# Fourth quarter of Q by seven-product runs, reciprocals of the attention denominator spread earlier, six output stores issued by ScalarE

## The chip, the cores and the metric

The kernel runs on one core of one Trainium2 chip. A core has five engines that run their own instruction streams in order: TensorE (PE; its weight loads are shown as PEld), VectorE (DVE), ScalarE (ACT), GpSimd (POOL) and SyncE (SP). They share an on-chip memory (SBUF), a set of accumulation banks that PE writes (PSUM) and 16 DMA engines. The metric is the device time of one execution in microseconds, the median of several executions; lower is better.

## The reference, cut to what matters

The input x has 2048 tokens of 1024 features, in bfloat16. The first block is linear attention with 32 heads of 32 features after a layer norm; the second is a token mixer, a two-layer MLP over the token axis with 3584 hidden units.

```python
def _A_ref(x, wqkv, wo):                       # x is layer-normed
    qkv = ((x @ wqkv).reshape(B, S, 3, H, Dh)).transpose(2, 0, 3, 1, 4)
    q, k, v = qkv[0], qkv[1], qkv[2]
    phi = lambda t: jnp.where(t > 0, t + 1, jnp.exp(t)) + 1e-6
    pq, pk = phi(q), phi(k)
    kv = jnp.einsum("bhsd,bhse->bhde", pk, v)
    z = jnp.einsum("bhsd->bhd", pk)
    num = jnp.einsum("bhqd,bhde->bhqe", pq, kv)
    den = jnp.einsum("bhqd,bhd->bhq", pq, z)[..., None] + 1e-6
    return (num / den).transpose(0, 2, 1, 3).reshape(B, S, D) @ wo
...
h = x + _A_ref(_layernorm(x), A_wqkv, A_wo)
h2 = h + _B_ref(_layernorm(h), B_w1, B_b1, B_w2, B_b2)   # norm, w1 over tokens, gelu, w2, transpose
```

So each token's phi(q) is needed, and a reciprocal of one denominator per token and head.

## The kernel before, in words

All large products use a seven-product scheme for two-by-two blocks (in the manner of Strassen and Winograd): four products' worth of sums of blocks are made on DVE, and PE does seven block products in place of eight. Where it isn't used, a plain product is done.

**Keys, values, queries.** The tokens are taken in eight pairs of 128 (`q` from 0 to 7). For each pair there is a key run and a value run (`KRun`, `VRun`): seven products of four matmuls of 512 columns each. `run_step` interleaves a run with the end of the previous one. The queries are kept transposed, 1024 features by tokens, in `pqT`; the tokens are cut in four quarters `u` of 512, and the features in eight groups `j` of 128. One *unit* (u, j) is a plain product: eight matmuls of 512 columns, then phi, which is an exponential and a relu on ACT and two instructions on DVE (`phi_evac`). Quarter 2 alone is done by two seven-product runs (`QRun`, halves 0 and 1), set between the key and value runs of pair 5; each of their seven products is eight matmuls of 256 columns. The other 24 units are plain: eight of them are placed among the key and value runs and right after them (`q_fill`), the other 16 in the loop over `q_units[8:]`.

**The loop over the left units.** With index n it does one unit a pass (`q_held`), and beside it: `kv_transpose` and `fold(j)`, which multiply the key-value matrix of each head into the output weights `wo_sb` (two matmuls a pass, evacuated by ACT and DVE); `den(u)`, eight small matmuls whose result is the denominators of a quarter, then a logarithm and an exponential on ACT, which write the reciprocals into the one buffer `rd_sb`, and a store of it to DRAM (`rd_dram`); `den_spread(u)`, eight DMAs that read it back, each to 32 partitions, four for the half h=0 of the features and four for h=1, into one of three buffers (`thirds`); `scale_q(u, h)`, one DVE instruction that multiplies phi(q) of half a quarter by the reciprocals; and the first sums of the mixer (`first_sums`), which need the mixer's first weights (`load_w1(0, ...)`, two loads of 1 MB). The dictionaries `den_at`, `spread_at`, `scale_at` and `sums_at` say at which n each stands.

**The output blocks.** For each of the 16 blocks of 128 tokens, `seed(i+1)` copies x into two PSUM banks, `out_mm(i)` adds sixteen matmuls of 512 columns (its weights are the scaled `pqT`), and `out_evac(i)` copies the sum to SBUF, takes the statistics of the next layer norm on DVE and stores the block. `h_scale`, `normalize_h` and `combine_h` prepare the mixer's operands. A block's eight weight loads for j = 0 to 7 come in order, j = 0 to 3 from the half h=0 of a quarter, j = 4 to 7 from h=1.

**What sets the order.** Most of this stretch is written out by hand (`pin`, and the wrappers `hv`, `ht`, `hs`, `hd`, which hold an instruction of DVE, PE, ACT or SP in program order). The rest is placed by a scheduler at build time. In the compiled order every DMA that SP or ACT issues gets one of eight completion counters (DMAHW0 to DMAHW7), given out in turn over both queues in the scheduler's order; a DMA isn't issued before the previous DMA on its counter has landed, and until then all that follows on its queue waits too.

Of the kernel before, what the change touches and what calls it, by code (L numbers as in the profile page):

```python
# [10 lines left out]
P = 128  # L11
# [19 lines left out]
def kernel(  # L31
# [751 lines left out]
    with ExitStack() as actx:  # L783
# [26 lines left out]
        with ExitStack() as a1:  # L810
# [11 lines left out]
            later = [pqT[:, j:j + 4, u * SW:(u + 1) * SW].bitcast(FP16) for u, j in ((1, 0), (NSC - 1, 0), (NSC - 1, 4))]  # L822
# [485 lines left out]
            q_units = [(u, j) for u in (0, 1, NSC - 1) for j in range(ND)]  # L1308
# [28 lines left out]
            for q in range(2, NVP):  # L1337
                runs = [KRun(q), VRun(q)]
                if q == 5:
                    runs = [runs[0], QRun(q // 2, 0), runs[1], QRun(q // 2, 1)]  # L1340
                for n in runs:
# [11 lines left out]
                    def after5():  # L1353
                        if kind == "V":
                            kv_accum(2 * q - 2)
                            kv_accum(2 * q - 1)
                        if i < NS:
                            ln_finish(i)
                            load_next(i + 2)

                    def after7():
                        if kind == "V" and q != 5 and q + 1 < NVP:
                            x_sums(q + 1)
                        if kind == "Q" and n.half == 1:
                            x_sums(q + 1, slice(0, 3))
# [10 lines left out]
            q_fill()  # L1376
            kv_accum(NS - 2)
            kv_accum(NS - 1)
            for n in range(3):
                q_fill()  # L1380
# [29 lines left out]
        ndp = a3p.enter_context(tc.tile_pool(name="ndp", bufs=3, space=PSUM))  # L1410
        rd_dram = [dram.tile([P, SW], FP16, name=f"rd_dram{u}") for u in range(NSC)]

        with ExitStack() as a3:
# [17 lines left out]
            SPREAD = (0, 2, 1, 3)  # L1431
            NH = ND // 2

            def den_mm(u):
                ps = ndp.tile([P, SW], F32, tag="den", name="den_ps")
                for o in range(2):
                    for g in range(4):
# [5 lines left out]
                            start=(o == 0),  # L1443
                            stop=(o == 1),
# [5 lines left out]
            def den_inv(u, ps):  # L1450
                hs.activation(ps[:], ps[:], ACT.Ln, bias=eps_den[:], scale=1.0 / S)
                hs.activation(rd_sb, ps[:], ACT.Exp, scale=-1.0)
                hd.dma_start(rd_dram[u][:], rd_sb)

            def den_spread(u):
                rows = rd_dram[u].rearrange("(g o h) n -> o h g n", g=4, h=HB)
                for h in range(2):
# [8 lines left out]
            def den(u):  # L1466
                den_inv(u, den_mm(u))
# [37 lines left out]
            def place(i):  # L1505
                u, r = divmod(i, NSC)
                return i if u != 2 else NSC * u + r % 2 * 2 + r // 2

            def out_mm(i):
                at = place(i) * P  # L1510
                for dc in range(NDC):
# [10 lines left out]
            def out_evac(i):  # L1522
# [8 lines left out]
                hd.dma_start(o_dram[i * P:(i + 1) * P, :], h_bf[:])  # L1531
# [17 lines left out]
            for half in range(2):  # L1549
                load_w1(0, half, pin)  # L1550
            for i in range(XRL + 1):
                load_xr(i)

            def first_sums():
                cur = Quad([Mixer1(0), Mixer1(1)])
                for m in (5, 6, 7, 3):
# [4 lines left out]
                Held.on = False  # L1561
                yield cur
# [3 lines left out]
            sums_at, ahead = (4, 8, 9, 11, 13), first_sums()  # L1566
            scale_at = {5: (0, 0), 6: (0, 1), 10: (2, 0), 12: (2, 1), 15: (1, 0)}
            den_at = {0: 0, 2: 2, 9: 1}
            spread_at = {0: 0, 6: 2, 12: 1}
            kv_transpose()  # L1570
            for n, (u, j) in enumerate(q_units[8:]):
                if n == len(q_units) - 8 - 1:
                    seed(0)
                q_held(u, j)
                if 1 <= n < 1 + ND:
                    fold(n - 1)
                if n in den_at:
                    den(den_at[n])
                if n in spread_at:
                    den_spread(spread_at[n])  # L1580
                if n in (12, 13):
                    load_w1(1, n % 2, pin)
                if n in scale_at:
                    scale_q(*scale_at[n])
                if n in sums_at:
                    cur = next(ahead)
# [10 lines left out]
            scale_at = {0: (1, 1), 6: (3, 0), 8: (3, 1)}  # L1597
# [243 lines left out]
```

## Time and profile before

| | |
|---|---|
| median of 3 runs | 558.95 us (558.83 to 558.98) |
| profiled execution | 559.43 us, of which the instructions span 557.7 us |
| busy share of the span | PE 99%, DVE 80%, PEld 57%, ACT 52%, POOL 5% |
| chain that ended last | PE 91%, DMA 4%, DVE 2%, ACT 1% |
| loop over the 16 left units | 143.3 to 177.2 us |
| output blocks | 177.2 to 233.1 us |
| granted clock | 1.0 of full speed throughout |

The span is cut at times counted from its first instruction. A busy share is an average over stages; a stage is read from its own windows. The start of a matmul group, less the start of the group before it, is the time that the earlier one held PE (the durations printed overlap, since matmuls are pipelined).

### The profile page before, as it was taken

How to read it: one execution, taken by the hardware profiler on the slowest of the kernel's cores; microseconds unless marked ns; L12 is line 12 of the kernel's file. 1: busy time of each engine (PE TensorE's matmuls, PEld its weight loads, DVE VectorE, ACT ScalarE, POOL GpSimd, SP SyncE). 2: the span in 40 equal slices, each digit the busy share in tenths (PEclk: the TensorE clock that was granted, in tenths of full speed). 3: DMA queues.
4: the chain of work that ended last, by engine and by line, in shares of the span. 5: the costliest groups of instructions: out<-in, count | busy, mean ns of one | idle time of the engine just before them, and what ended most of it. 6: DMA issues, size and time to landing. Idle time of an engine off the chain costs nothing.

```text
span 557.7 us, 8915 instructions
## 1 busy us (share of the span) xinstructions
PE 550.7 (99%) x3370; PEld 320.4 (57%) x3387; DVE 443.8 (80%) x858; ACT 288.8 (52%) x614; POOL 26.2 (5%) x36
## 2 busy tenths in 40 slices
PE   8999999999999999999999999999999999999997
PEld 3444446645444444456766767666444667667665
DVE  6898888754488688889989789887996879749747
ACT  5747678665776877646556465464210412413311
POOL 1000000000000000000000000000003103103111
PEclk9999999999999999999999999999999999999999
DMA  8933341202966961102250440413769659849434
GB/s 297 308 76 76 80 89 22 39 0 72 317 155 192 316 196 75 76 0 90 64 152 4 148 133 21 150 43 91 202 204 237 190 137 242 209 126 240 94 106 75
DMA packets 83931, 74.51 MB, mean 134 GB/s; under 512 B 15650, under 2 KB 76336, under 8 KB 83888
## 3 DMA queue, kind: packets, MB, share of 16 engines
q1 hardware_dynamic: 79504, 69.87, 42.0%
q0 software_dynamic: 4096, 3.68, 5.0%
q8 instruction: 26, 0.43, 0.3%
q10 hardware_dynamic: 288, 0.39, 0.2%
q14 instruction: 17, 0.14, 0.1%
HBM read 59.12 MB, written 11.67 MB: 127 GB/s over the span
## 4 chain that ended last, share of the span: by engine, by line
PE 91%; DMA 4%; DVE 2%; ACT 1%; SPq 1%; issue 0%; DVEq 0%; ACTq 0%
PE psI L234 23%; PE psC L234 14%; PE acc_t L234 14%; PE psB L234 8%; PE psC L966 4%; PE psB L966 4%; PE psA L966 4%; PE acc_t L888 3%; PE acc_t L1298 2%; PE psB L346 2%; PE psA L346 2%; PE psE L966 2%; PE psC L346 2%; DMA wq<-in_B_w_dram 2%; DMA wkv<-in_A_wqkv_dram 1%; PE kvps L917 1%
## 5 line engine op out<-in xcount | busy, mean ns | idle before, releaser
L234 PEld LDWEIGHTS <-is 128*128 128x128 f16 x736 | 71.8, 98 | 31.3 <-DVE is L234 0.4
L234 PEld LDWEIGHTS <-sa 128*128 128x128 f16 x606 | 59.2, 98 | 27.5 <-issue 0.3
L234 PEld LDWEIGHTS <-wq 128*128 128x128 bf16 (+1 forms) x496 | 48.5, 98 | 28.1 <-issue 1.2
L234 PE MATMUL acc_t<-wo_sb,pqT 128*128 128x512 f16 x256 | 55.6, 379 | 0.0
L491 POOL DMA_DIRECT2D out_dram<-wq x28 | 24.3, 927 | 519.6 <-ACT wq L494 487.7
L234 PEld LDWEIGHTS <-pqT 128*128 128x128 bf16 x256 | 25.0, 98 | 30.5 <-issue 0.6
L234 DVE TENSOR_TENSOR t<-psI,t 128x256 f32<-128x256 f32 (+1 forms) x45 | 20.8, 475 | 22.2 <-PE psI L234 21.0
L194 DVE TENSOR_SCALAR e_sb<-e_sb 128x512 bf16<-128x512 bf16 x64 | 18.4, 287 | 21.8 <-ACT e_sb L189 21.6
L234 PE MATMUL psC<-gs,wq 128*128 128x512 f16 x140 | 34.1, 379 | 0.0
L966 PEld LDWEIGHTS <-xs 128*128 128x128 f16 x208 | 20.1, 98 | 22.1 <-DVE xs L955 0.6
L234 PE MATMUL psC<-hT,sa 128*128 128x512 f16 x112 | 31.2, 379 | 0.0
L234 PE MATMUL psI<-hi,is 128*128 128x256 f16 x200 | 30.0, 273 | 0.0
L234 PE MATMUL psB<-hT,sa 128*128 128x512 f16 x112 | 29.7, 379 | 0.0
L234 PE MATMUL acc_t<-xnT,wq_sb 128*128 128x512 bf16 x125 | 29.3, 379 | 0.3
L189 ACT ACTIVATE e_sb<-acc_t 128x512 bf16<-128x512 f32 x32 | 19.1, 598 | 18.6 <-PE acc_t L1298 10.0
L234 DVE BATCH_NORM_STATS2 hst<-acc_t 128x6 f32<-128x512 f32 x32 | 21.4, 691 | 9.1 <-ACT h_bf L234 8.9
L966 PE MATMUL psA<-wkv,xnT 128*128 128x512 bf16 x98 | 26.2, 379 | 0.3
L966 PEld LDWEIGHTS <-xnT 128*128 128x128 bf16 x156 | 15.2, 98 | 18.1 <-issue 0.2
L234 PE MATMUL psC<-hT,wq 128*128 128x512 f16 x96 | 24.6, 379 | 0.0
L234 ACT CAST h_bf<-acc_t 128x512 bf16<-128x512 f32 x32 | 18.4, 582 | 12.0 <-PE acc_t L234 12.0
L234 DVE TENSOR_TENSOR e<-psI,es 128x256 f32<-128x256 f32 x20 | 8.5, 424 | 19.9 <-PE psI L234 19.9
L234 ACT COPY psI<-psI 128x256 f32<-128x256 f32 x50 | 18.0, 360 | 11.7 <-PE psI L234 9.8
(246 smaller groups left out, 1131.6 us busy)
## 6 DMA issues: line engine op xcount, KB each, us to landing
wq<-in_B_w_dram SPq DMA_DIRECT2D x14, 1024.0 KB, 7.9
wq<-in_B_w_dram SPq DMA_DIRECT2D x12, 896.0 KB, 7.6
gs<-parked SPq DMA_DIRECT2D x9, 896.0 KB, 4.7
shared_sb<-rd_dram SPq DMA_DIRECT2D x32, 128.0 KB, 3.9
out_dram<-h_bf SPq DMA_DIRECT2D x16, 256.0 KB, 2.0
x_sb<-in_A_x_dram SPq DMA_DIRECT2D x14, 256.0 KB, 3.0
w2o<-in_B_w_dram SPq DMA_DIRECT2D x4, 896.0 KB, 11.3
out_dram<-wq POOLq DMA_DIRECT2D x28, 128.0 KB, 4.6
```

The costliest lines, as they stand in the source:

```text
L189: pin(nc.scalar.activation(e_sb[:], src, ACT.Exp))
L194: pin(nc.vector.tensor_scalar(e_sb[:], e_sb[:], 1.0, PHI_EPS, ALU.min, ALU.add))
L234: return (lambda *a, **kw: pin(op(*a, **kw))) if self.always or getattr(Held, self.key) else op
L346: pe.matmul(ps[:, cols], lhsT=lhs[:, k, :], rhs=mv(k)[:, cols], start=(start and k == 0), stop=(k == self.nk - 1), skip_group_check=True,)
L491: nc.gpsimd.dma_start(to, ot[:, a:b], accum_op=ALU.add)
L888: mm = nc.tensor.matmul(pp[:, 0:CW], lhsT=xnT[:, kt, i * P:(i + 1) * P], rhs=wkv[:, kt, c * CW:(c + 1) * CW], start=(kt == 0), stop=(kt == ...
L917: pin(nc.tensor.matmul(kv_ps[b][:, sl, :], lhsT=pks[i % NPK][:, j * P:(j + 1) * P], rhs=vaugs[i % NVA][:, j, :], start=False, stop=(i == N ...
L966: pin(nc.tensor.matmul(ps[:], lhsT=lhs[:, k, :], rhs=rhs[:, k, :], start=(start and k == 0), stop=(k == hk2 - 1), skip_group_check=True,))
L1298: nc.tensor.matmul(qp[:, 0:SW], lhsT=wq_sb[:, kt, j * P:(j + 1) * P], rhs=xnT[:, kt, u * SW:(u + 1) * SW], start=(kt == 0), stop=(kt == ND ...
```

## The change

It has five parts.

1. Quarter 3 of the queries is done by two more `QRun`s, after the value run of pair 7, in place of eight plain units. One plain fill stays there, so that four plain units are spent before the loop and 12 are left for it (`q_left`: units 0 to 3 of it are (0, 4) to (0, 7), units 4 to 11 are (1, 0) to (1, 7)). Three of the buffers for sums move within `pqT` to places that are free then.
2. In the loop the order of the quarters becomes 2, 0, 3, and a half of 1: `den_at`, `spread_at`, `scale_at` and `SPREAD` are rewritten. `kv_transpose` comes after unit 0 rather than ahead of it.
3. The denominators of quarter 1 are done in two halves: the first four groups at n = 9 into a DRAM buffer of their own (`rd_half`), the other four within output block 0. To make that possible two strips of `zz` are set to S by DVE at n = 7.
4. The stores of the reciprocals and of output blocks 0 to 5 are issued by ACT (`hs`) in place of SP (`hd`).
5. On SP's queue the mixer's first weights and the first two loads of x come after the spread of quarter 2; the second pair of mixer weights moves from n = 12 and 13 to output blocks 8 and 9. The sums of the mixer that stood at n = 4, 8, 9, 11, 13 are at n = 8 and 11 and at output blocks 5, 9 and 11.

```diff
-            q_units = [(u, j) for u in (0, 1, NSC - 1) for j in range(ND)]
+            q_units = [(u, j) for u in range(2) for j in range(ND)]
...
+                elif q == NVP - 1:
+                    runs += [QRun(q // 2, 0), QRun(q // 2, 1)]
...
+                        if kind == "Q" and q == NVP - 1 and n.half == 1:
+                            kv_accum(NS - 2)
+                            kv_accum(NS - 1)
...
             run_step(None, prev, fill=q_fill)
-            q_fill()
-            kv_accum(NS - 2)
-            kv_accum(NS - 1)
-            for n in range(3):
-                q_fill()
+            q_left = list(q_next)
...
-            SPREAD = (0, 2, 1, 3)
+            SPREAD = (2, 0, 1, 3)
+            TURN = 9
...
-            def den_mm(u):
+            def den_mm(u, os=(0, 1)):
                 ps = ndp.tile([P, SW], F32, tag="den", name="den_ps")
-                for o in range(2):
+                for o in os:
...
-            def den_inv(u, ps):
+            def den_inv(ps, to):
                 hs.activation(ps[:], ps[:], ACT.Ln, bias=eps_den[:], scale=1.0 / S)
                 hs.activation(rd_sb, ps[:], ACT.Exp, scale=-1.0)
-                hd.dma_start(rd_dram[u][:], rd_sb)
-
-            def den_spread(u):
-                rows = rd_dram[u].rearrange("(g o h) n -> o h g n", g=4, h=HB)
-                for h in range(2):
+                hs.dma_start(to[:], rd_sb)
+
+            def den_spread(u, halves=(0, 1)):
+                for h in halves:
+                    rows = (rd_half if (u, h) == (1, 0) else rd_dram[u]).rearrange("(g o h) n -> o h g n", g=4, h=HB)
...
-                hd.dma_start(o_dram[i * P:(i + 1) * P, :], h_bf[:])
+                (hs if i < 6 else hd).dma_start(o_dram[i * P:(i + 1) * P, :], h_bf[:])
...
-            for half in range(2):
-                load_w1(0, half, pin)
-            for i in range(XRL + 1):
-                load_xr(i)
...
-            sums_at, ahead = (4, 8, 9, 11, 13), first_sums()
-            scale_at = {5: (0, 0), 6: (0, 1), 10: (2, 0), 12: (2, 1), 15: (1, 0)}
-            den_at = {0: 0, 2: 2, 9: 1}
-            spread_at = {0: 0, 6: 2, 12: 1}
-            kv_transpose()
-            for n, (u, j) in enumerate(q_units[8:]):
+            sums_at, ahead = (8, 11), first_sums()
+            scale_at = {6: (2, 0), 7: (2, 1), 9: (0, 0), 10: (0, 1)}
+            den_at = {1: 2, 4: 0, 6: NSC - 1, 9: 1}
+            spread_at = {3: 2, 6: 0, 11: 1}
+            for n, (u, j) in enumerate(q_left):
...
                 q_held(u, j)
+                if n == 0:
+                    kv_transpose()
...
+                if n == 7:
+                    for at in (0, 2 * HB):
+                        hv.memset(zz[:, :, at:at + HB], float(S))
                 if n in den_at:
-                    den(den_at[n])
-                if n in spread_at:
-                    den_spread(spread_at[n])
-                if n in (12, 13):
-                    load_w1(1, n % 2, pin)
+                    den(den_at[n], (0,) if den_at[n] == 1 else (0, 1))
                 if n in scale_at:
                     scale_q(*scale_at[n])
+                if n in spread_at:
+                    den_spread(spread_at[n], (0,) if spread_at[n] == 1 else (0, 1))
+                    if n == 3:
+                        for half in range(2):
+                            load_w1(0, half, pin)
+                        for i in range(2):
+                            load_xr(i)
+                    if n == 6:
+                        for i in range(2, XRL + 1):
+                            load_xr(i)
...
+                if n == TURN:
+                    for _ in range(4):
+                        acc_ring.append(acc_ring.pop(0))
...
-            scale_at = {0: (1, 1), 6: (3, 0), 8: (3, 1)}
+            scale_at = {0: (1, 0), 2: (1, 1), 6: (3, 0), 8: (3, 1)}
             for i in range(NS):
                 seed(i + 1)
-                out_mm(i)
                 if i == 0:
                     load_xr(XRL + 1)
-                    den(NSC - 1)
-                    for k in range(XRL + 2, XRL + XR2 + 1):
+                    out_mm(0, (0,))
+                    den(1, (1,))
+                    load_xr(XRL + 2)
+                    den_spread(1, (1,))
+                    out_mm(0, (1,))
+                    for k in range(XRL + 3, XRL + XR2 + 1):
                         load_xr(k)
-                if i == 2:
+                else:
+                    out_mm(i)
+                if i == 4:
                     den_spread(NSC - 1)
+                if i in (8, 9):
+                    load_w1(1, i % 2, pin)
+                if i in (5, 9, 11):
+                    cur = next(ahead)
```

## The prediction

> **What bounds the kernel now.** I read the page's busy shares first, then the windows of the changed stretch, then PE's timeline for gaps, then the queues behind the one gap that I found.
>
> ```profile
> PE 550.7 (99%) x3370; PEld 320.4 (57%) x3387; DVE 443.8 (80%) x858; ACT 288.8 (52%) x614; POOL 26.2 (5%) x36
> ```
>
> ```profile
> 143.00:177.00 34.00, 33.37 (x174) 14.51 (x175) 24.92 (x50) 25.68 (x48) 0.00 (x0) 1.00 0.67 193
> 181.30:233.00 51.70, 51.70 (x244) 23.48 (x241) 42.64 (x88) 38.11 (x91) 0.00 (x0) 1.00 0.52 174
> ```
>
> PE bounds everything: less PE work counts in full, and a new PE gap counts in full too, as nothing later can make it up. Of the two windows the first is the loop over the left units, the second the output blocks (columns: window, its length, then busy time and count of PE, PEld, DVE, ACT, POOL, the granted clock, DMA share, GB/s). The loop lacks 0.63 us of PE. PE's timeline shows where:
>
> ```profile
> 90.63 1.04 PE L1103 MATMUL psE<-xs,shared_sb 128*128 128x256 f16 x8
> 91.50 1.04 PE L1103 MATMUL psC<-xs,pqT 128*128 128x256 f16 x8
> ...
> 152.81 1.89 PE L234 MATMUL acc_t<-xnT,wq_sb 128*128 128x512 bf16 x8
> 154.54 0.38 PE L234 MATMUL acc_t<-wo_sb,kvT 128*128 128x512 bf16 x1
> 155.29 0.38 PE L234 MATMUL acc_t<-wo_sb,kvT 128*128 128x512 bf16 x1 [0.37 <-ACT r_sb L191]
> 155.76 1.89 PE L234 MATMUL acc_t<-xnT,wq_sb 128*128 128x512 bf16 x8
> ```
>
> Start to start, one product of a Q run (eight matmuls of 256) holds PE 0.87 us, and a plain unit (eight of 512) 1.73. A fold matmul takes 0.22, so 154.54 to 155.29 holds a gap of 0.53 and 155.29 to 155.76 one of 0.25. ACT's and SP's timelines, and the landing times (last column), say why:
>
> ```profile
> 146.91 0.60 ACT L234 ACTIVATE shared_sb<-den_ps 128x512 f16<-128x512 f32 x1
> 153.66 0.60 ACT L234 ACTIVATE shared_sb<-den_ps 128x512 f16<-128x512 f32 x1 [1.76 <-DMA rd_dram<-shared_sb]
> ```
>
> ```profile
> 147.53 0.33 SPq L234 DMA_DIRECT2D rd_dram<-shared_sb  x1
> 168.62 0.34 SPq L234 DMA_DIRECT2D rd_dram<-shared_sb  x1
> 170.38 3.63 SPq L234 DMA_DIRECT2D shared_sb<-rd_dram  x8
> ```
>
> ```profile
> DMA to landing us min/median/max: 3.1/3.6/6.1
> ```
>
> ```profile
> rd_dram<-shared_sb SPq DMA_DIRECT2D x1, 128.0 KB, 1.7
> ```
>
> The reciprocals have one SBUF buffer. The first store of it went out behind 3 MB of loads and took 6.05 us (147.53 to 153.58 in the chain of waits); ACT sat 1.76 us before the next exponential, and PE then for ACT. The store at 168.62 found idle DMA engines and landed in 1.7. The row transfers at 170.38 took 3.1 us for the first and 3.6 in the median.
>
> One more view matters for the new order, SP's own waits while the last spread is issued, at 189.5 to 195.2:
>
> ```profile
> SPq L234 <- DMA xr<-in_A_x_dram: 2.0, 4, 0.9
> SPq L234 <- DMA shared_sb<-in_A_x_dram: 0.7, 2, 0.4
> SPq L234 <- DMA out_dram<-h_bf: 0.6, 2, 0.4
> ```
>
> The eight rows wait for loads and stores that have nothing to do with them: each waits for the landing of the DMA eight places earlier, which holds its completion counter. Here this costs nothing, as quarter 3 is needed some 20 us later.
>
> **The change part by part.**
>
> *Quarter 3 by runs.* Eight plain units, 8 x 1.73 = 13.8 us, become 14 products, 14 x 0.87 = 12.2: -1.6 us. Two Q runs in a row ask of ACT three copies, four evacuations and two exponentials each, nine times 0.5 us of 6.1, and of DVE some 4.6; covered by PE's 6.1 (beside the Q runs near 90 and 104 us PE shows no gap above 0.25).
>
> A rule speaks against this part. The Trainium skill, "TensorE: Matmul & The Clock Gate", section "Back-to-back issue gap", gives about 131 ns for a sustained matmul of 512 columns and 81 for one of 128, the weight load setting the pace of the short ones. By that the eight units cost 64 x 0.131 = 8.4 us and the runs at least 112 x 0.081 = 9.1, a loss of 0.7 or more, and my sum would end 2.3 us higher. The trace has 216 and 109 ns, so I go by the trace.
>
> *The old gap.* Stores and exponentials are now two or three passes apart: -0.53 - 0.25 = -0.8 us.
>
> *kv_transpose after unit 0.* ACT's copy of it (1.02 us) now stands behind unit 0's exponential and relu: unit end + 0.20 + 0.49 + 0.48 + 1.02 = 2.19 us. PE gets to the fold after 0.45 of transposes and a unit of 1.73, 2.18. With a wake-up and a weight load PE waits 0.1 to 0.2: +0.15.
>
> *Denominators in five blocks, not four.* Each block has about 0.09 us of PE gap ahead of it: +0.1.
>
> *The spread of quarter 0, where the new wait is.* In the changed kernel's compiled order SP and ACT draw the eight counters together, so the rows of quarter 0 stand behind ACT's stores:
>
> ```
> SP   51 shared_sb<-rd_dram0 [waits DMAHW1_49]   2nd row; counter last used by ACT's store of quarter 3
> SP   53 shared_sb<-rd_dram0 [waits DMAHW3_49]   4th row; by the first mixer weights
> SP   55 shared_sb<-rd_dram0 [waits DMAHW5_49]   6th row; by ACT's store of rd_half
> PE 2078 acc_t<-wo_sb,pqT x 8 [waits DVE_49] @4 [waits DVE_49]   output block 0: at matmuls 0 and 4 its weight loads wait for scale_q(0,0) and (0,1)
> ```
>
> Rows 6 to 8 belong to the half h=1, and scale_q(0, 1) needs them; the fifth weight load of output block 0 needs that. But rd_half is made from a den that stands after unit 9. From the end of unit 9: ACT 0.20 later starts the exponential; exponential, relu, logarithm, exponential take 0.49 + 0.48 + 0.71 + 0.62, so the store starts at +2.50 (in the trace, unit end 166.12 to store 168.62 is 2.50 by the same steps); it lands 1.7 later, +4.2; SP issues three rows at about 0.45 each, the third at +5.1; it lands 3.1 to 3.6 later, +8.2 to +8.7; the multiply takes 1.2 with its wake-ups (1.21 is the row of scale_q): +9.4 to +9.9. PE without the wait: half a den 0.37, units 10 and 11 at 1.73, four matmuls 0.87: it asks at +4.7. So PE stands still for 4.7 to 5.2 us. If the engines are busy, the store takes 3.6 to 3.8 (its other rows, 6.05 the most) and rows 4.6 (the first spread): up to 8. By then the mixer's weights have landed, so I take the near end, +5.0. Behind the waiting multiply DVE holds the phi of unit 11 and sums; nobody on PE needs them sooner. A gain from this wait is excluded: PE did not wait here.
>
> *Moved on SP's queue.* The mixer's first weights go out about 161 to 162.5 us and land 8 to 11 later (their rows: 8.8 and 11.4, then 8.5 and 10.9), 171 to 174. DVE's first mixer sum waits for them to 174, which can hold scale_q(0, 0) till 177; row 2 of the spread, held till quarter 3's store lands near 170, does the same. Both end before the 181 at which scale_q(0, 1) is done; with that cover gone they would cost up to 1.6. The second pair, issued near 210, is first read near 247: 0. The loads of x are read two passes or more after landing: 0.
>
> *DMA issues on ACT.* ACT's two at the start take 0.41 and 0.45 us. In the loop five more; a pass with a den asks 3.3 us of ACT in 2.8 of PE, the next gives 0.7 back. In the output blocks ACT needs 2.6 of 3.46 us a block, 3.0 with a store. Hidden: 0; if not, at most 6 x 0.45 = 2.7. Here a page bears: "DMA: Bandwidth & Descriptors", "Issuing engines are not separate DMA queues", says that another issuing engine saves only the issuing time, as all run on the same 16 DMA engines. No row here shows ACT storing under load, and my sum doesn't need it.
>
> *Mixer sums among the output blocks.* DVE gets 1.13 + 1.6 + 1.13 us more in blocks 5 to 11 and one scale (1.13) in block 0. It idles 0.34 + 0.81 us in two blocks; it falls behind by about 2 us and recovers by the end. PE asks for a freed bank some 5 us after the statistics: 0, at worst +1.
>
> **Sum.** -1.6 - 0.8 + 0.15 + 0.1 + 5.0 = +2.85. On the profiled 559.43 (span 557.7 and 1.73 around it) that is 562.3; the median of the runs is 0.48 lower, so 561.8.
>
> **Rivals.**
>
> *The counters don't bind* (faster). If rows 6 to 8 go out with the others near 173, PE finds quarter 0 scaled: -1.6 - 0.8 + 0.25 = -2.15, 556.8. For it: PE at 99%, the old gap is real. Against: SP's waits above. It decides when the multiply ends by +6.9 after unit 9, 2.5 us sooner than my least chain.
>
> *Stores under load* (slower still). The store of quarter 0 goes out near 162.4 with 2 MB in flight; if it takes 6 us as the first one did, ACT is held before the next exponential for 1.7, PE for about 1, and the later rows take 4.6: +1 to +3, 563 to 565. Against: a queue of its own, which no row shows.
>
> *DVE becomes the bound in the output blocks*: +1, 562.8. For: its 42.64 of 51.70 us, with 5 us added. Against: the banks' slack.
>
> **How the numbers follow.** The main case 0.66 (own range 561.3 to 562.8), counters that don't bind 0.13, stores under load 0.14, DVE 0.07. Range 560.4 to 564.2: it leaves out the fast case and the upper part of the loaded one. Faster or slower counts from 0.2%, 1.1 us, about what the measurement can tell from no change: faster 0.13, same 0.03, slower 0.84.
>
> **What would show it.** PE's row of output block 0 broken after four matmuls by about 5 us, ended by DVE's multiply; SP idle before the sixth row until rd_half lands; no 1.76 us wait of ACT; 14 products of 0.87 before the loop. Wrong if the block runs through, or if the break is at its first matmul (then the rows before, or the weights, were the later ones).

## The result and the profile after

The changed kernel takes 571.71 us (median of four runs, 570.64 to 572.27), the kernel before 558.89 (558.70 to 558.98): 2.28% slower, a ratio of 1.0228 with a 95% interval of 1.0210 to 1.0245. The forecast was 561.8. The direction is right and the wait that it named is there, 5.02 us where 5.0 were added (two errors cancel in it, as told below), but the loss is 12.8 us and not 2.85. The profiled execution took 571.40 us with a span of 569.6, 11.9 more than before.

First the page: PE's busy share is down from 99% to 97%, and the row of the granted clock, all nines before, has a 7 and an 8 at slices 13 and 14, 171 to 199 us.

```profile
PE 552.9 (97%) x3418; PEld 325.3 (57%) x3435; DVE 447.7 (79%) x864; ACT 291.9 (51%) x618; POOL 26.3 (5%) x36
...
PEclk9999999999997899999999999999999999999999
```

PE's timeline of that stretch (start, duration, what; in brackets the idle time before it and what ended it) has three long gaps, and after two of them the rows are too long:

```profile
169.19 0.38 PE L234 MATMUL acc_t<-wo_sb,kvT 128*128 128x512 bf16 x1
171.29 0.38 PE L234 MATMUL acc_t<-wo_sb,kvT 128*128 128x512 bf16 x1 [1.72 <-ACT r_sb L191]
171.77 2.91 PE L234 MATMUL acc_t<-xnT,wq_sb 128*128 128x512 bf16 x8
174.62 0.62 PE L234 MATMUL den_ps<-pqT,zz 128*32 128x512 bf16 x4
175.16 3.97 PE L234 MATMUL acc_t<-xnT,wq_sb 128*128 128x512 bf16 x15
180.17 1.04 PE L234 MATMUL acc_t<-wo_sb,pqT 128*128 128x512 f16 x4 [1.04 <-DVE pqT L234]
186.23 1.89 PE L234 MATMUL acc_t<-wo_sb,pqT 128*128 128x512 f16 x4 [5.02 <-DVE pqT L234]
```

The 5.02 us at the fifth weight load of output block 0 is the forecast wait. The gaps at 171.29 and 180.17 are not in the sum. And the unit that starts at 171.77 takes 2.85 us to the next group, where every unit before took 1.73. The windows say why (third number from the end: the granted clock):

```profile
172.50:175.80 3.30, 3.30 (x12) 0.86 (x11) 3.20 (x5) 1.77 (x5) 0.00 (x0) 0.50 0.11 29
...
186.30:189.40 3.10, 3.10 (x10) 0.75 (x11) 1.64 (x3) 0.65 (x1) 0.00 (x0) 0.50 1.01 221
190.00:236.00 46.00, 46.00 (x215) 20.86 (x214) 40.99 (x81) 33.58 (x79) 0.00 (x0) 1.00 0.67 215
```

PE is busy through both of the first two, at half clock. The third is the rest of the output blocks, 46.00 busy of 46.00: nothing is lost there. The chain in order of time names the causes, and ends with the mixer's first product, which started at 233.30 before:

```profile
162.25 6.77 DMA rd_dram<-shared_sb
...
177.02 2.73 DMA rd_half<-shared_sb
179.77 0.30 SPq L234
...
180.59 4.24 DMA shared_sb<-rd_dram
...
184.95 1.24 DVE pqT L234
...
242.75 6.91 PE psA L234 x32
```

So 9.45 us of the 11.9 are lost by the mixer's start (233.30 to 242.75). The store of quarter 0's reciprocals took 6.77 us, and ACT's timeline shows that the next exponential waited for it:

```profile
165.86 0.70 ACT L234 ACTIVATE den_ps<-den_ps,eps_den 128x512 f32<-128x512 f32 x1
169.10 0.60 ACT L234 ACTIVATE shared_sb<-den_ps 128x512 f16<-128x512 f32 x1 [2.54 <-DMA rd_dram<-shared_sb]
```

The other 2.45 us come in the second layer. Of them 1.9 are one stop of PE: its matmul of 482.45 is followed by one at 484.56, because DVE's sums wait for a load of weights. The rest is two shorter stops behind it, 0.4 near 492 and 0.3 near 525 us, which no run followed up.

```profile
483.23 0.62 DVE L234 TENSOR_TENSOR is<-wq 128x896 f16<-128x896 bf16 x1 [2.26 <-DMA wq<-in_B_w_dram]
```

The kernel before has no such gap. There the two loads in question are issued 9.4 us sooner, as all the work around them is, but they take 5.7 and 8.5 us where they now take 7.7 and 11.1.

### The profile page after: what moved, and what is told of

The parts are those of the page before. It is cut to its first block, busy times and chain, and to the rows that moved or that the text cites. A ratio compares the mean times of both kernels' runs of the same rounds, so it can differ in the third digit from the quotient of the medians.

```text
span 569.6 us, 9025 instructions
## 1 busy us (share of the span) xinstructions
PE 552.9 (97%) x3418; PEld 325.3 (57%) x3435; DVE 447.7 (79%) x864; ACT 291.9 (51%) x618; POOL 26.3 (5%) x36
## 4 chain that ended last, share of the span: by engine, by line
PE 86%; DMA 7%; DVE 4%; ACT 1%; issue 1%; ACTq 0%; SPq 0%; DVEq 0%
PE psI L234 20%; PE psC L234 13%; PE acc_t L234 12%; PE psB L234 8%; PE psC L966 4%; PE psA L966 4%; PE psB L966 4%; DMA wq<-in_B_w_dram 4%; PE acc_t L888 3%; PE psB L346 2%; PE psA L346 2%; PE psE L966 2%; PE psC L346 2%; DVE is L234 1%; PE kvps L917 1%; PE psA L1103 1%
## 5 line engine op out<-in xcount | busy, mean ns | idle before, releaser
L234 PE MATMUL acc_t<-wo_sb,pqT 128*128 128x512 f16 x256 | 57.1, 385 | 6.1 <-DVE pqT L234 6.1
L234 PE MATMUL psI<-gi,is 128*128 128x256 f16 x168 | 22.3, 273 | 2.0 <-DVE is L234 2.0
L234 PE MATMUL acc_t<-xnT,wq_sb 128*128 128x512 bf16 x93 | 23.6, 396 | 0.4 <-issue 0.2
L234 ACT COPY psI<-psI 128x256 f32<-128x256 f32 x50 | 18.0, 360 | 11.6 <-PE psI L234 9.7
```

What stands on the lines that cost most here:

```text
L234: return (lambda *a, **kw: pin(op(*a, **kw))) if self.always or getattr(Held, self.key) else op
```

## The experiments

**The half denominator, two passes and one pass later.** In the changed kernel rows 6 to 8 of quarter 0 are issued when the store of `rd_half` lands. If its counter is the cause, a place where no row draws that counter must free them, and a later place on the same counter must hold them longer.

```diff
-            den_at = {1: 2, 4: 0, 6: NSC - 1, 9: 1}
+            den_at = {1: 2, 4: 0, 6: NSC - 1, 11: 1}    # and scale (1, 0) at output block 1
```

> One number of the changed kernel is moved: the half denominator of quarter 1 stands at n = 11 and not at n = 9 (its scale (1, 0) one block later). In the compiled order its store then comes among the rows of quarter 0, on a counter that none of rows 6 to 8 draws. Theory A (the rows were late because their counter was held by that store): PE's 5.02 us wait at the fifth weight load of output block 0 shrinks to some 1 to 1.5 us, since the rows still can't go before the store of quarter 3 has landed and their buffer is free; with it goes the stretch at half clock behind the wait (3.4 us at half speed, 1.7 us lost). From 571.7: about 566, 565 to 568, with the 2.1 us gap near 169 still there. Theory B (the rows were late because the DMA engines were busy with loads of x and the mixer's weights): the wait stays about 5 us and the time 571 to 572.

567.09 us (566.23 to 569.22), ratio 1.0160. PE's timeline:

```profile
180.49 1.04 PE L234 MATMUL acc_t<-wo_sb,pqT 128*128 128x512 f16 x4 [1.34 <-DVE pqT L234]
183.85 1.89 PE L234 MATMUL acc_t<-wo_sb,pqT 128*128 128x512 f16 x4 [2.33 <-DVE pqT L234]
```

The same edit with `10: 1`:

> The same move by one pass only, to n = 10: the compiled order keeps rd_half on the counter that the sixth row of quarter 0 draws, but the store starts one unit (1.73 us) later while PE asks for quarter 0 at the same time. Theory A (counter): the 5.02 us wait grows to about 6.8, the time to about 573.4 (572.8 to 574.5). Theory B (busy DMA engines): no change, 571 to 572.

571.35 us (570.30 to 573.86).

```profile
188.22 1.89 PE L234 MATMUL acc_t<-wo_sb,pqT 128*128 128x512 f16 x4 [6.19 <-DVE pqT L234]
```

The wait goes from 5.02 to 2.33 with the counter free, and to 6.19 with the store one pass later. In this second run the sixth row is issued at 181.38, 0.01 us after `rd_half` has landed (179.77 and 179.75 in the changed kernel). That settles the counter. The median of the second run doesn't show the longer wait and lies where the rival, busy DMA engines, had put it: its runs scatter over 3.6 us, and the store found idle engines (1.70 us in place of 2.73). The profile decides between the two. What is left of the wait in the first run, 2.33, is the rows behind quarter 3's store, 175.21 to 182.45. Its time was as expected, but not in the expected way: the wait was to shrink to 1 or 1.5 us and the half clock behind it to go. In its profile the clock is low as long as in the changed kernel, 6.83 us, and PE now works through 5.5 of them and not 3.3. So of the 2.7 us of wait that are gone 1.1 come back as slow matmuls.

**A second buffer for the reciprocals.**

```diff
+    rd2_sb = xctx.enter_context(tc.tile_pool(name="rd2pool", bufs=1)).tile([P, SW], FP16, name="rd2_sb")
...
+            rd_ring = [rd_sb, rd2_sb[:]]
...
+                rd_ring.append(rd_ring.pop(0))
+                rd = rd_ring[-1]
...
-                hs.activation(rd_sb, ps[:], ACT.Exp, scale=-1.0)
-                hs.dma_start(to[:], rd_sb)
+                hs.activation(rd, ps[:], ACT.Exp, scale=-1.0)
+                hs.dma_start(to[:], rd)
```

> The reciprocals get a second SBUF buffer, taken in turn; all else is as in the changed kernel, the 6.77 us store of quarter 0 beside 2 MB of loads too. Theory C (ACT is held because the next exponential needs the one buffer, and PE then waits for ACT): the gaps of 2.10 and 0.25 us near 169 to 172 go, and with them the 3.4 us at half clock that follow (1.7 us). PE then reaches the end of unit 9 about 3.3 us earlier; the chain to the fifth weight load of output block 0 hangs on that unit's end (+11.6 us in the trace), so the whole 3.3 is gained: about 568.4, 567 to 569.5. Rival D (ACT is held by issuing DMAs into a busy queue, not by the buffer): the gaps stay and so does the time, 571 to 572.

568.67 us (566.88 to 569.62), ratio 1.0178. The store still takes 6.84 us, but ACT no longer waits and the gap near 169 is gone. PE's timeline from there:

```profile
168.48 1.89 PE L234 MATMUL acc_t<-xnT,wq_sb 128*128 128x512 bf16 x8
170.21 0.59 PE L234 MATMUL acc_t<-wo_sb,kvT 128*128 128x512 bf16 x2
170.64 1.89 PE L234 MATMUL acc_t<-xnT,wq_sb 128*128 128x512 bf16 x8
...
179.87 1.23 PE L234 MATMUL acc_t<-wo_sb,pqT 128*128 128x512 f16 x4 [3.46 <-DVE pqT L234]
184.57 1.89 PE L234 MATMUL acc_t<-wo_sb,pqT 128*128 128x512 f16 x4 [3.46 <-DVE pqT L234]
```

So the single buffer made that gap. The time is 3.0 us less, as expected, but again not in the expected way. The gap and its stretch at half clock are gone, but the rows are hardly sooner, so the first weight load waits 3.46 us where it waited 1.04, and the fifth 3.46 where it waited 5.02. And the clock behind them stays low for 10.24 us in place of 6.83, from 180.58 to 190.82:

```profile
190.00:190.50 0.50, 0.50 (x3) 0.20 (x2) 0.17 (x1) 0.00 (x0) 0.00 (x0) 0.50 0.00 0
191.00:191.50 0.50, 0.50 (x4) 0.25 (x3) 0.32 (x1) 0.15 (x1) 0.00 (x0) 1.00 0.23 70
```

Counted from quarter 3's denominators (164.75 and 165.76) the fifth weight load comes 2.7 us sooner, and the mixer only 1.2. The profiled executions differ by 1.9: the rest is a start that was 1.0 longer and a second layer that was 1.7 shorter, where DVE's wait for the load is 1.4 in place of 2.26. That the time came out as expected was luck, as far as this profile tells.

**The loads back ahead of the loop.**

```diff
+            for half in range(2):
+                load_w1(0, half, pin)
+            for i in range(XRL + 1):
+                load_xr(i)
...
-                    if n == 3:
-                        for half in range(2):
-                            load_w1(0, half, pin)
...
-                            load_xr(i)
```

> The mixer's first weights and the four first loads of x go back ahead of the loop, where the kernel before had them; the rest of the change stays. Now the store of quarter 2 (two passes in) meets the 3 MB of loads, but three passes lie between it and the next exponential; the store of quarter 0 near 162 finds the engines nearly idle and should take 1.7 to 3 us, not 6.77. In the compiled order the turn of the counters shifts too: rd_half holds a counter that no row of quarter 0 draws; the fourth row draws that of quarter 3's store. So by theories A and C both large gaps of PE and both stretches at half clock go, about 2.35 + 1.7 + 1.0 + 5.0 + 1.7 = 11.8 us less: 560 to 561.5. If the loads beside the store were not the cause, the gap near 169 stays and the time is about 564 to 566.

559.85 us (557.78 to 561.43, eight runs), ratio 1.0019 (1.0003 to 1.0035). The granted clock is 1.0 throughout. PE's timeline:

```profile
175.70 1.02 PE L234 MATMUL acc_t<-wo_sb,pqT 128*128 128x512 f16 x4 [0.50 <-ACT acc_t L234]
177.22 1.04 PE L234 MATMUL acc_t<-wo_sb,pqT 128*128 128x512 f16 x4 [0.49 <-DVE pqT L234]
```

One edit takes back 11.9 of the 12.8 us. The store of quarter 0 takes 4.44 us, three passes lie between the slow store (now quarter 2's, 5.67 us) and the next exponential, and the turn of the counters puts `rd_half` where no row waits for it. This run alone does not separate the counter from the buffer; the three above do.

**What an idle PE costs by itself.** Six stalls in the kernel before, with no DMA moved:

```diff
+            def stall(k):
+                ps = ndp.tile([P, SW], F32, tag="den", name="den_ps")
+                for t in range(2):
+                    ht.matmul(ps[:, 0:SW], lhsT=wo_sb[:, 0, 0:P], rhs=pqT[:, 0, 0:SW], start=True, stop=True)
+                    if t == 0:
+                        for _ in range(k):
+                            hs.copy(ps[:], ps[:])
```

> The kernel before, with six artificial stalls of PE and nothing else: a matmul, k copies of its bank on ACT (k = 1, 2, 3 after the units n = 4, 7, 11 of the loop; k = 2, 4, 6 after output blocks 4, 8, 12), then a matmul that needs the copies. No DMA is moved. It measures what an idle PE costs beyond the idle time. A copy is some 0.5 us and ACT is first done with its own work, so the stalls should be about 1.4 to 3.5 us, 15 us in all with the twelve matmuls. Theory E (the half clock follows from PE's idle time alone): behind the longer stalls, from 1.7 to 2 us of idle on, the granted clock is 0.5 for about 3.4 us, each costing 1.7 us; total 579 to 584. Rival F (the half clock in the changed kernel came from something else of that stretch, such as DMA traffic): the granted clock stays 1.0 and the time is about 574 to 576.

581.03 us (579.39 and 582.67), 22.0 above before. PE's timeline has two short matmuls for each stall, with the stall between them; the rows are the second matmul of the fourth stall, then both of the fifth and both of the sixth. After them come the windows behind the fifth, in the sixth and behind it (the third number from the end is again the granted clock):

```profile
205.28 0.38 PE L234 MATMUL den_ps<-pqT,wo_sb 128*128 128x512 bf16 x1 [1.26 <-ACT den_ps L234]
219.30 0.38 PE L234 MATMUL den_ps<-pqT,wo_sb 128*128 128x512 bf16 x1
222.15 0.38 PE L234 MATMUL den_ps<-pqT,wo_sb 128*128 128x512 bf16 x1 [2.46 <-ACT den_ps L234]
236.17 0.38 PE L234 MATMUL den_ps<-pqT,wo_sb 128*128 128x512 bf16 x1
240.22 0.59 PE L234 MATMUL den_ps<-pqT,wo_sb 128*128 128x512 bf16 x1 [3.67 <-ACT den_ps L234]
```

```profile
222.20:225.60 3.40, 3.40 (x17) 1.51 (x17) 2.93 (x5) 2.79 (x7) 0.00 (x0) 1.00 0.20 77
238.70:240.20 1.50, 0.00 (x0) 0.00 (x0) 0.00 (x0) 1.44 (x4) 0.00 (x0) 0.50 0.00 0
240.30:245.40 5.10, 5.10 (x13) 1.79 (x13) 2.44 (x5) 2.84 (x7) 0.00 (x0) 0.50 0.15 55
```

Only the longest stall lost the clock, for 6.83 us; stalls of 2.10, 2.65 and 2.46 us did not. So idle time alone does it, but my rule, that a certain length is enough, is wrong. The clock's records give a better one: it changes only at steps of 3.41 us (the low stretches behind waits last 3.41, 6.83 or 10.24 us in all runs), and what counts is how much of one such step PE was idle. Worked out from the starts of the matmuls: 2.05 us of idle in one step (the fifth stall) kept the clock, 2.14 lost it (the gap near 169 of the changed kernel, 1.88 + 0.26). Nothing between the two was measured. A stall that straddles two steps and leaves less than that in each costs only itself, as the third here, 2.65 us, and the one at 482 in the changed kernel.

**Where the late gap comes from.** First a place in DRAM, then the changed kernel without its extra buffer:

```diff
-        rd_dram = [dram.tile([P, SW], FP16, name=f"rd_dram{u}") for u in range(NSC)]
+        rd_dram = [dram.tile([P if u else 2 * P, SW], FP16, name=f"rd_dram{u}")[0:P] for u in range(NSC)]
```

> The kernel before with 128 KB more of DRAM set aside in front of its buffers (the first rd_dram twice as large, half of it unused), as rd_half does in the changed kernel. Nothing else moves. Theory G (the gap of 2.1 us near 482, absent before, comes from the place of the later DRAM buffers, since the same load there took 5.7 us before and 7.7 after): the load takes about 7.5 us, the gap of about 2 us appears near 473, and the time is 1.5 to 2 us above before. Rival H (it comes from the order of the DMAs or their counters): no change, within 0.3 us of before.

558.53 us (558.11 to 559.54), ratio 0.9995 (0.9986 to 1.0004); no gap.

```diff
-        rd_half = dram.tile([P, SW], FP16, name="rd_half")
+        rd_half = rd_dram[2]        # on top of the loads ahead of the loop
```

> The changed kernel with the loads back ahead of the loop, as in the run that gave 559.85, and rd_half put into rd_dram[2], which is free by then, so that DRAM holds the same buffers as in the kernel before. Theory G: the gap of 1.9 us near 472 goes and the time is 558 (557.3 to 558.7). Rival H: no change, 559 to 560.5. In either case two short gaps of PE (about 0.65 us each) remain ahead of output block 0, since DVE does a mixer sum of 1.22 us before the two scales.

559.82 us (557.77 to 561.38), the gap at 472 still there. The place in DRAM is not it. The landing records show more: a load lands in sixteen parts, and in the kernels with the gap fifteen of the first load's land as in before and one 1.5 to 2.9 us later. In the same stretch the trace has a transfer of 16 KB of PE's instructions, one for every 256 or so:

```
                    first load: issued, 15th, 16th part   second load: 15th, 16th   PE fetch at
before              460.38  466.07  466.08                471.12  471.16            470.60
changed             469.82  475.09  477.50                480.40  483.20            470.59
loads ahead         459.30  464.54  466.76                469.81  472.45            460.08
+100 PE instr.      459.75  464.94  466.92                470.08  472.60            460.38
ahead, +40 instr.   460.18  465.48  465.52                470.51  470.65            456.86
```

The changed kernel has 6873 PE instructions in its compiled order, before 6776, so the fetch moves against the load. The test is to add PE instructions to the kernel before and nothing else:

```diff
         for t in range(n):
-            mm(warm[:, 0:P], warm[:, 0:BANK])
+            for c in range(6):
+                mm(warm[:, 0:P], warm[:, 0:BANK // 6])
```

> The kernel before; the ten matmuls of 512 columns with which PE bridges the first loads are each cut into six of 85 columns, so that PE's instruction stream has 100 instructions more (6876, the changed kernel 6873, before 6776) and all that follows is as it was. Theory I (the gap near 482 comes from PE's instruction fetch: a transfer of 16 KB every 256 PE instructions, which in every profile with the gap starts within the load of the second layer's weights and holds one of its sixteen parts up by 2 to 3 us, and in the two without it doesn't): the fetch moves from 470.6 to about 463, one part of the load lands 2 to 3 us after the other fifteen, a gap of about 2 us comes up near 473, and the time is 1.5 to 2 us above before (plus up to 1 us if the start of the kernel is held up). Rival K (the gap comes with the order or number of the DMAs, which don't change here): the load takes 5.7 us as before, no gap near 473, and the time is that of before but for the start.

560.02 us (558.16 to 560.87), ratio 1.0014 (1.0000 to 1.0028): 1.3 us more by the medians, 0.8 by the ratio, whose interval just reaches no change, and less than the 1.5 to 2 expected. Three of the twelve runs lie at 558.2 to 558.6 and nine at 559.3 to 560.9. The profile is what shows it: from the mixer's start on it is 1.3 us longer than before's. The gap is there, in DVE's timeline as in the changed kernel, and the DMA queues from 459.8 to 467.0 show the one fetch:

```profile
472.62 0.63 DVE L235 TENSOR_TENSOR is<-wq 128x896 f16<-128x896 bf16 x1 [1.73 <-DMA wq<-in_B_w_dram]
```

```profile
q1 hardware_dynamic: 2999, 1.73, 87.4%
q8 instruction: 1, 0.02, 0.8%
```

And the other way round, `range(3)` in the kernel with the loads ahead:

> The changed kernel with the loads back ahead of the loop (559.85), the ten first matmuls cut into three each: 40 more PE instructions, so that each fetch comes some 3 us sooner, the one at 460.1 before the load of 459.3 starts. Theory I: the gap of 1.9 us near 472 goes, 558.0 (557.3 to 558.6). Rival K: no change, 559.3 to 560.5.

558.90 us (558.43 to 560.15), the late gap gone. The time is above the expected range (557.3 to 558.6), since PE has a new gap of 0.7 us that ends at 43.42: here a fetch at 37.5 falls into a load of transposed tokens, which takes 4.79 us in place of 3.16. So the count of PE instructions decides whether the late gap is there. How a fetch that itself takes about 1 us holds one part up by 2 to 3 was not tried, and it doesn't always: in the profile of `repaired_2` below the fetch fell into the load at 460.77 and the sixteenth part was 0.5 us late.

**Is the rest of the account complete?** If the seven-product runs and the old gap do gain 2.4 us, a version without the losses must show it.

```diff
+            # loads ahead of the loop; denominators of quarter 3 in output block 2, spread and scales
+            # one block later; first mixer sum in output block 3; rd_half = rd_dram[2]
+            den_at = {1: 2, 4: 0, 9: 1}
+            sums_at, ahead = (11,), first_sums()
```

> The last kernel with the two remaining waits taken out: the denominators of quarter 3 move from n = 6 to output block 2 (their store held the counter of the fourth row of quarter 0; spread and scales one block later), and the mixer sum at n = 8 moves to output block 3, out of the way of DVE's scales. If my account is complete (part 1 gains 1.6, the old gap 0.8, nothing else is left), PE runs through into output block 0 and the time is about 1.9 to 2.2 us below before: 556.4 by theory G, 558.3 by H. If quarter 0 is still late, 557.5 to 559.

563.72 us (562.65 to 565.61). This order computes quarter 3's denominators after `zz` has been overwritten, so its outputs of that quarter are other numbers; the instructions and their times are those described. The expectation failed: with one sum more, DVE falls behind in the output blocks, and the mixer's first product starts 3.04 us after the matmul at 232.93, and the clock is lost for 3.4. That is the third rival of the prediction, which the changed kernel escapes.

```diff
+            # loads ahead; second buffer
+            den_at = {1: 2, 4: 0, 5: NSC - 1, 9: 1}
+            sums_at, ahead = (10, 11), first_sums()
```

> The loads back ahead of the loop, a second buffer for the reciprocals, the denominators of quarter 3 one pass sooner (n = 5, so that their store has landed when the rows of quarter 0 draw its counter) and the mixer sum of n = 8 moved behind DVE's two scales (n = 10). The two waits of 0.65 us ahead of output block 0 should go or shrink to 0.3, the gap near 472 stays: 558.5 to 559. If quarter 0 is still late, 559.5 to 560.5.

559.78 us (558.46 to 560.90), above the expected 558.5 to 559. The three waits ahead of and within output block 0 stay: 0.66, 0.25 and 0.68 us.

> The last kernel with the 40 PE instructions more at the start. If my account of the change is complete (1.6 by the runs, 0.8 by the old gap, and each loss named), this leaves nothing but those gains: 556.5 to 557.3. If the gap near 472 has another cause, as repaired_2.

558.86 us (558.54 to 560.31): 2 us above what I expected. Its profile has them: 0.66, 0.25 and 0.67 us of waits at output block 0, and 0.5 at 43 us, where a fetch at 37.1 falls into the load of transposed tokens as in the run with 40 instructions above. (The next expectation still puts this down to the start.)

```diff
+            den_at = {1: 2, 4: 0, 5: NSC - 1, 11: 1}     # repaired_3; 9: 1 in repaired_3_n9
+            sums_at, ahead = (4, 11), first_sums()
...
-        for t in range(n):
-            mm(warm[:, 0:P], warm[:, 0:BANK])
+        for t in range(n if n < 6 else 4 * n):
+            mm(warm[:, 0:P], warm[:, 0:BANK if n < 6 else BANK // 4])
```

> The changed kernel with the loads back ahead of the loop, a second buffer for the reciprocals, the denominators of quarter 3 at n = 5, the half of quarter 1 at n = 11 (its scale one block later), the first mixer sum at n = 4, where DVE is idle for 1.75 us, and only the first six matmuls cut into four (36 PE instructions more, with no time of their own). In the run repaired_2_40_pe three waits of 0.66, 0.25 and 0.67 us were left (ACT's copies of x for output block 0 stood behind the half denominator's logarithm, exponential and store; a mixer sum stood before DVE's last phi) and a start 0.7 us longer. If these were all that hid the gains of the runs (1.6) and of the old gap (0.8): 556.3 to 557.0, the gap near 472 absent. If those gains aren't there: 558 to 559.

560.37 us (559.58 to 560.62): 3.4 above the upper end of what I expected. Quarter 1's second half comes too late (0.69 us, at 193.84), so does DVE's scale of quarter 0 (0.51, at 178.72), and the gap near 43 is there, 0.7 us. The profiled execution also started 1.1 us later than that of the next run.

> As repaired_3, but the half of quarter 1 stays at n = 9. In the compiled order no row of quarter 0 draws its counter, so a difference between the two shows what ACT's 1.75 us there cost by themselves: the 0.66 us wait for the copies of x comes back, 557.0 to 557.7. If it costs nothing, as repaired_3.

558.57 us (558.14 to 559.72), 0.9 above the expected 557.0 to 557.7, also with a gap at 42.5 of 0.86 from start to start. It is the other fetch: moved from 43.9 to 37.3, it falls into the load of transposed tokens issued at 35.2, which takes 4.6 us in place of 3.1 (36.3 and 4.8 in `repaired_3`). A fetch that is moved out of one load had been moved into another. With 24 instructions more instead of 36 (the first six matmuls cut into three):

> repaired_3_n9 with the first six matmuls cut into three in place of four: 24 PE instructions more than the changed kernel and not 36. There a fetch at 37.3 fell into the load of the first transposed tokens (36.3; 4.8 us in place of 3.1) and PE waited 0.6 us at 43.4 for it, which none of the kernels without the extra instructions does. With 24 the fetch should come near 40, after that load, and the later one near 458, ahead of the load of 459.3: both gaps gone, 557.8 to 558.1. If the wait at 43 has another cause, 558.4 to 558.7.

557.93 us (557.33 to 559.87), as expected, before beside it 558.70: ratio 0.9986 (0.9974 to 0.9998). Both gaps are gone. The page and PE's timeline:

```profile
PE 549.3 (99%) x3430; PEld 326.8 (59%) x3447; DVE 447.4 (80%) x864; ACT 292.0 (52%) x618; POOL 26.2 (5%) x36
```

```profile
171.91 3.63 PE L234 MATMUL acc_t<-xnT,wq_sb 128*128 128x512 bf16 x15
176.04 2.15 PE L234 MATMUL acc_t<-wo_sb,pqT 128*128 128x512 f16 x8 [0.51 <-ACT acc_t L234]
```

Its mixer starts at 231.99, before's at 233.13: 1.2 us sooner from the end of the start on (30.68 and 30.62), with 0.9 still lost at output block 0 (0.67 ahead of its first matmul, 0.25 ahead of its fifth). So the gains are there: with these 0.9 they are 2.1 of the 2.15 that the prediction had for its first four terms together. This version is faster than the changed kernel, and than the one before by 0.14%, less than the 0.2% that the forecast took as measurable; the interval only just leaves out no change.

```diff
-                if n == len(q_left) - 1:
+                if n == len(q_left) - 3:
                     seed(0)
```

> repaired_4, and ACT's copies of x for output block 0 two passes sooner, ahead of the half denominator. If ACT's order is what makes the 0.66 us wait at the first matmul of output block 0, it goes to 0.1 to 0.3, the second wait grows by 0.2 to 0.4 (DVE's scale of h=1 is not sooner), and the time is 557.4 to 557.9. If the wait is DVE's, no change against repaired_4.

560.64 us (560.06 to 561.67), worse by 2.7: PE waits 0.9 and 0.9 us for ACT within the loop, probably as the copies of x hold two accumulation banks two passes longer, and DVE is late at the mixer's start (1.99 from start to start). The remaining wait can't be bought off that way.

## Why the prediction was right in direction and wrong in size

The step that failed is the sum. It put the stores under load at 0, as a rival in place of the counter wait, where they came on top of it (+2.1, and +1.2 at the first weight load). It priced idle time of PE at the idle time alone, where half clock behind it cost +3.3 more. And it had nothing for the second layer (+2.45). The counter wait that the sum did have was right.

Term by term, in us, against the profiled execution of the changed kernel:

| step of the prediction | forecast | measured |
|---|---|---|
| quarter 3 by runs | -1.6 | -1.6 (products 0.87 apart, no gap) |
| the old gap | -0.8 | -0.8 there, but the same wait came back at 169 |
| kv_transpose after unit 0 | +0.15 | 0 (26 matmuls without a break from 148.31) |
| denominators in five blocks | +0.1 | +0.1, and one 0.16 of issue |
| the spread of quarter 0, second half | +5.0 | +5.2 |
| its first half ("up to 1.6 if that cover is gone") | 0 | +1.2 |
| rival: stores under load | 0 (+1 to +3) | +2.1 |
| DMA issues on ACT; mixer sums | 0 | 0 (46.00 of 46.00) |
| half clock after the two long gaps | not in it | +1.7 and +1.6 |
| instruction fetch in the second layer | not in it | +2.45, of which 1.9 the gap |

The measured ones add up to 12.1; the spans differ by 11.9.

*The spread of quarter 0* was the right step by the right mechanism: the counter, the third row, the fifth weight load. Two of its terms were off and cancelled: the chain from the end of unit 9 took 11.6 us and not 9.4 to 9.9 (the store 2.73 for 1.7, the row 4.24 for 3.1 to 3.6), but PE also asked later, for it ran at half clock and had waited for the first half.

*Stores under load* was treated as a rival at 0.14, its direct cost priced right (6 us for the store, ACT held, 1 to 3 in all) and set aside for one reason: ACT has a queue of its own. The runs settle that: issued from ACT, the store takes 6.77 us beside 2 MB of SP's loads and 1.70 to 1.72 on idle engines. That is what the rule cited there says, in the Trainium skill, "DMA: Bandwidth & Descriptors", section "Issuing engines are not separate DMA queues". The prediction quoted it and then said that its sum did not need it. It did: this case was no alternative to the counter wait but came on top of it, and belonged in the sum.

*The cover of scale_q(0, 0)* was named, and its price if gone: up to 1.6. It went, for 1.2, because quarter 3's store, too, ran under load: it started at 169.73, took 4.76 us, and the second row of quarter 0, held by its counter, was issued at 174.51, 0.02 us after it had landed. The prediction had that landing near 170.

*The clock* is the failure of method: every idle microsecond was priced at one, while an idle stretch of more than some 2.1 us within one 3.41 us step makes PE run the next step at half speed. The prediction's own 5 us gap was bound to have this cost, since wherever it falls it leaves at least 2.5 us in one step. The Trainium skill, "TensorE: Matmul & The Clock Gate", section "What's actually happening", tells of windows of about 3.4 us that run freely; the trace agrees (3.41). It puts the loss of the clock after a whole idle window, and the section "HAM oscillation — how this bites in real kernels" warns of gaps above 3.4 us; here 2.14 us in one window was enough, so the measurement decides.

*The late gap* is in no row of the kernel before, and nothing in that stage was changed. The number of PE instructions that the change adds (97) was in the compiled order, though.

## What to carry to other kernels

Rivals that act at different places are not alternatives: add their prices, and ask of each wait what it makes late next. Here a PE gap of more than about 2 us within one step cost the gap and 1.6 to 3.1 us of speed behind it, so the stretch at half clock belongs in the price; and a gap that is shortened but still loses the clock gives back less than it was shortened by. When a stage that nobody touched gets slower, look at which part of which transfer lands last, and what else is fetched then; a change of a hundred instructions can move a microsecond or two there, in either direction.

## What the hardware showed that I had not expected

- The granted clock changes in steps of 3.41 us: down to 0.5 after a step with 2.14 us of idle PE or more, not after one with 2.05; back to 1.0 after a step that PE filled but for 0.4 us at most. Less idle keeps it low than brings it down: with the second buffer PE stood still for the first 0.58 us of a low step (183.99 to 184.57), and the next step was low too.
- A fetch of 16 KB of PE's instructions, about every 256 of them, that starts within a load can delay one of the load's sixteen parts by 1.5 to 2.9 us, and with it all who wait for the load. Adding 100 PE instructions at the start of the kernel before made a gap at 472, 1.6 us from start to start.
- A 128 KB store from ACT's queue took 1.7 us alone, 4.4 to 5.9 beside row transfers and loads of x, 6.8 to 7.4 beside 2 MB of weights.
